# Reordering the split-precision products of a routed feed-forward by kind, and counting several column blocks per product in its routing searches

## The chip, the cores and the metric

The kernel runs on one core of one Trainium2 chip. The metric is the device time of one execution in microseconds, as the median of several runs. The profile and its trace come from one execution, profiled apart from those runs.

## What is computed

Three stages follow each other: causal attention mixed with a memory read-out, a routed feed-forward with eight experts, and a second feed-forward with weights common to all tokens. Cut to what matters, the reference is:

```python
x = attention(q, k, v, M_prev, z_prev, beta)      # 2304 tokens x 512
logits = x @ w_gate                               # 8 experts, 288 places each
order = np.argsort(-logits.flatten())
for idx in order:                                 # best pair of token and expert first
    tok, e = (int(idx) // E, int(idx) % E)
    if assigned[tok] >= 0 or counts[e] >= cap:
        continue
    assigned[tok] = e
    counts[e] += 1
for e in range(E):
    h = np.maximum(x[assigned == e] @ w1[e], 0.0)
    out[assigned == e] = h @ w2[e]
h = np.maximum(np.maximum(x @ w1, x @ w2), x @ w3)   # x is now that out
return h @ w_out
```

## The kernel before

Every matmul of the two feed-forwards has float32 accuracy from three products that add up in one accumulator: an fp32 product of the rounded halves ("hi", line 1429) and two bf16 products with the rests ("lo", lines 1431 and 1432). `mm3` issues the three together, so that TensorE goes hi, lo, lo, hi, lo, lo. Weights are split on the fly: ScalarE rounds (`whi`, line 1370), VectorE subtracts (`wlo`, line 1376), ScalarE copies the rounded half as bf16 (line 1380). The common weights are split once into `mh` and `ml` (lines 1280 to 1295).

The experts are worked through in the order in which they fill up, p = 0 to 7, 288 tokens each. For one expert the kernel gathers its token rows (line 1345), transposes them (line 1405) and splits them. The first feed-forward goes over eight blocks fb of the hidden layer: four triples over d into an accumulator `w` (task "h1", lines 1451 to 1460), a ReLU and a split into `hh` and `hl`, and four triples into the accumulators `acc` (task "y", lines 1480 to 1493). The last two blocks' y products are made together. The second feed-forward (lines 1521 to 1595) goes over six blocks f: three tiles i of four triples each from `yh` and `yl`, of which the maximum `mt` is kept (line 1552), then the output products (`fo`), 512 columns wide. Three accumulators `w` exist.

Between these products runs the routing (`routing`, line 1043). Which expert fills up next, and with which tokens, is found by a search per expert: VectorE compares each token's best logit with a grid of thresholds (`cq`, line 1140), TensorE counts by expert how many tokens lie above each threshold, one product per column block of 128 tokens, 18 in all (line 1148), VectorE compares the counts with the places left (`fl`, line 1152), TensorE sums the flags (line 1158), and VectorE moves the grid (lines 1167 and 1169). `PLANS` has the bits of each step: five steps (7, 5, 5, 5, 6) in the first search, four of 7 bits in the six later ones; the last expert needs none. A search ends with the expert's number (line 1181) and its token list (line 1225); the list is written to memory and read back in another layout on SyncE's queue (`fi` and `fj`, lines 1512 and 1516), which also issues the weight loads `wraw` (line 1361), three buffers deep.

The order on every engine is laid down before the run. `Plan.run` (line 151) takes tasks greedily: the one that can start first by planned costs and latencies, and among equals the one with the smaller key. The keys come from the tables `FK`, `RKEY` and `R1KEY`.

Of the kernel before, what the change touches and what calls it, by code (L numbers as in the profile page):

```python
# [22 lines left out]
F32 = mybir.dt.float32  # L23
# [18 lines left out]
PLANS = ((7, 5, 5, 5, 6), (7, 7, 7, 7))  # L42
# [3 lines left out]
RKEY = (-1000, -23.5)  # L46
FL0 = 3
NFILL = 88
R1, R1KEY = 9, 21.8
NK = 4  # L50
RSLACK = 300
# [4 lines left out]
FK = {"m2": -600, "ml": 28.3, "load": -63.7, "w2": 17.1, "wsplit": -3.5, "gather": -148.1, "xt": -126.2, "h1": 0, "y": -46.8, "o": 13.0, "store": 103.5, "idx": -41.5}  # L56
# [185 lines left out]
def attention(g, tc, ctx, consts, beta, qN, kN, v1, vT, mz, mT, wg, xd, L, m2):  # L242
# [677 lines left out]
    def search():  # L920
# [40 lines left out]
        op("DVE", 65, lambda: V.tensor_scalar(g.st[1], g.pw[1], g.am, None, op0=OP.mult), [t])  # L961
# [81 lines left out]
def routing(g, tc, plan, rt, rps, L):  # L1043
# [33 lines left out]
    es2 = tl("es2", [E])  # L1077
    k, key, slack = [0], [0.0], [0]

# [42 lines left out]
    for ph in range(E):  # L1122
# [7 lines left out]
        if ph < E - 1:  # L1130
            cur, cn = m, "m"
            pl = min(ph, 1)
            n = len(PLANS[pl])
            for s in range(n):
                Z, q, w = 2 ** PLANS[pl][s], CQ[pl], PQ[pl]
                late = ph == 0 and s == 0
                if late:
                    q = w = 3
                for a in range(CE if late else 0, NB, q):
# [10 lines left out]
                    P((30 if ph else 50) * w + (60 if ph else 0), cnt, " ".join(f"cq{x}" for x in range(a + q - w, a + q, q)) + " ohU" +  # L1150
                      (" CNT" if a + q > w or late else " RA"), "CNT")
                V(70, lambda Z=Z: v.tensor_tensor(fl[:Z], CNT[:Z], R[:Z], op=OP.is_ge), "CNT R", "fl")
# [7 lines left out]
                P((54 if base else 27) + 100 * (ph > 0), fpm, "fl", "FP")  # L1160
# [49 lines left out]
        for a in range(0, NB, q):  # L1210
# [10 lines left out]
            r.ti = P((30 if ph else 95) * w + (60 if ph else 0), idx, " ".join(f"cq{x}" for x in range(a + q - w, a + q, q)) + " mov0 mov1 mov2" +  # L1221
# [26 lines left out]
def experts(g, tc, plan, top, wr, xd, idxd, out):  # L1248
# [32 lines left out]
    for k in range(NK, 12):  # L1281
# [3 lines left out]
        def flow(e, k=k, h=0):  # L1285
            if h == 0:
                g.slot(k)
            q = slice(512 * h, 512 * h + 512)
            V.tensor_sub(ML[k][:, 0, q], g.W32[k][:, q], MH[k][:, q].bitcast(F32))

        t = add(FK["m2"] + k, {"ACT": act(1024)}, fh)
        for h in range(2):
            low = add(FK["ml"] + .1 * k + .05 * h, {"DVE": dve(512)}, lambda e, f=flow, h=h: f(e, h=h), [t, low, g.rounds[0].tt])
        low = add(FK["ml"] + .1 * k + .07, {"ACT": act(1024)}, lambda e, k=k: A.copy(ML[k][:, 1], MH[k].bitcast(F32)), [low])
# [36 lines left out]
    for p in range(E):  # L1331
# [95 lines left out]
        def mm3(o, w, r, start, stop, part=(0, 1)):  # L1427
            if 0 in part:
                nc.tensor.matmul(o, w[0], r[0], start=start, stop=False)  # L1429
            if 1 in part:  # L1430
                nc.tensor.matmul(o, w[2], r[1], start=False, stop=False)  # L1431
                nc.tensor.matmul(o, w[1], r[2], start=False, stop=stop)  # L1432

# [11 lines left out]
        ylast, yt = [], []  # L1445
        for fb in range(8):
# [4 lines left out]
            for hf in range(2):  # L1451
                def fh1(e, x=x, fb=fb, hf=hf, o=o):
                    if hf == 0:
                        o.pt = ps.tile([128, 512], F32, name="w", bufs=FBUFS["w"])
                    for d in (2 * hf, 2 * hf + 1):
                        s = slice(d * 128, d * 128 + 128)
                        mm3(o.pt[:, :T], wts(x.W[fb], s), tri(x.xh, x.xl, d), d == 0, d == 3)

                t = add(kh + FK["h1"] + .1 * hf, {"PE": 760}, fh1, x.tw[fb, 0] + (x.tx[:6] if hf == 0 else x.tx + [t]), new=[bp] if hf == 0 else [],
                        use=([] if hf == 0 else [bp]) + x.bx + list(x.bw[fb]))  # L1460
# [19 lines left out]
            for hf, (fb, ts, o, bhh, bhl) in itertools.product(range(2), yt):  # L1480
                def fy(e, x=x, fb=fb, hf=hf, o=o, part=(0, 1)):
                    for d in (2 * hf, 2 * hf + 1):
                        if fb == 0:
                            x.acc[d] = ps.tile([128, 512], F32, name="acc", bufs=4)
                        s = slice(512 + d * 128, 512 + d * 128 + 128)
                        mm3(x.acc[d][:, :T], wts(x.W[fb], s), (o.a, (o.b[:, 0] if 1 in part else None), (o.b[:, 1] if 1 in part else None)), fb == 0, fb == 7, part)

                ky = k0 + 2 * fb + FK["y"] + .1 * hf if fb < 6 else k0 + 14 + FK["y"] + hf + .1 * (fb - 6)
                for part in ((0,), (1,)) if fb == 7 else ((0, 1),):
                    ylast.append(add(ky + .05 * part[0], {"PE": 270 * (0 in part) + 490 * (1 in part)}, lambda e, f=fy, part=part: f(e, part=part),  # L1490
                                     list(ts if 1 in part else ts[:1]) + x.tw[fb, 1] + ylast[-1:] + ([o[-1] for o in prev.ol] if prev else []),
                                     new=ya[2 * hf:2 * hf + 2] if fb == 0 else [],
                                     use=[bhh, bhl] + list(x.bw[fb]) + (ya[2 * hf:2 * hf + 2] if fb else [])))
# [3 lines left out]
        for d in range(4):  # L1497
            def hi(x=x, d=d):
                if not hasattr(x, "yh"):
# [4 lines left out]
                               [ylast[-4 + d // 2 * 3]] + x.ty[:1], new=x.by if d == 0 else [], use=[ya[d]] + ([] if d == 0 else x.by)))  # L1504
# [13 lines left out]
        t = add(k0 + FK["idx"], {"SP": 500}, fi, [r.tt] + x.tl[FL0:FL0 + 1], lat=2300)  # L1518
        x.tidx = add(k0 + FK["idx"] + .1, {"SP": 500}, fj, [t], lat=2300)
        x.tm = []  # L1520
        for f in range(6):
# [3 lines left out]
            for i in range(3):  # L1525
# [3 lines left out]
                for hf in range(2):  # L1529
                    def fp(e, x=x, f=f, i=i, hf=hf, o=o, part=(0, 1)):  # L1530
                        if hf == 0 and 0 in part:
                            o.pt = ps.tile([128, 512], F32, name="w", bufs=FBUFS["w"])
                        for d in (2 * hf, 2 * hf + 1):
                            s = slice(d * F2 + f * 128, d * F2 + f * 128 + 128)
                            mm3(o.pt[:, :T], msub(i, s.start, 128), tri(x.yh, x.yl, d), d == 0, d == 3, part)

                    for part in ((0,), (1,)) if f == 0 and i == 0 else ((0, 1),):
                        need = x.ty[:6] if hf == 0 else x.ty + [t]
                        if part == (0,):
                            need = x.ty[6 * hf:6 * hf + 6:3] + ([t] if hf else [])  # L1540
                        elif part == (1,):
                            need = need + [t]
                        t = tp = add(kf + i + .1 * hf + .05 * part[0], {"PE": 270 * (0 in part) + 490 * (1 in part)},
                                     lambda e, f=fp, part=part: f(e, part=part), need + TM[i], new=[bp] if hf == 0 and 0 in part else [],
                                     use=([] if hf == 0 and 0 in part else [bp]) + x.by)
# [39 lines left out]
            for ci, c in enumerate(chunks):  # L1585
                h, w = (was, 0) if c * 128 < p * T else (own, 128 * (c - full[0]))

                def fo(e, x=x, f=f, ci=ci, h=h, w=w):
# [3 lines left out]
                    mm3(x.oc[ci], [a[:, w:w + 128] for a in (h.t, h.u[:, 0], h.u[:, 1])], msub(3, s.start, DM), f == 0, f == 5)  # L1592
# [121 lines left out]
```

## Time and profile before

| what | value |
|---|---|
| median of 3 runs | 817.12 us (816.01 to 817.22) |
| the profiled execution | 816.3 us |
| its span in the trace | 814.6 us |
| TensorE busy | 783.8 us, 96% of the span |
| VectorE, ScalarE, GpSimd busy | 578.6, 480.7, 107.6 us |
| granted TensorE clock, mean | 0.982 of full speed |
| HBM read, written | 72.77 MB, 9.74 MB |

Attention fills the span up to about 245 us, expert 0's gather begins at 263.6 us, and the last product starts at 807.0 us. Times are counted from the start of the span. Matmuls are pipelined, so the duration of one overlaps the next; the spacing of their starts says how long one holds the engine.

### The profile page before, as it was taken

To read this page: it belongs to the slowest core of one execution; us is meant where nothing else is said; L and a number is where in the kernel's file an instruction comes from. 1 tells how busy PE (TensorE), PEld (TensorE's weight loads), DVE (VectorE), ACT (ScalarE), POOL (GpSimd) and SP (SyncE) were. 2 spreads that over 40 slices of the span, in tenths; PEclk is the share of its full clock that TensorE was granted. 3 is DMA by queue.
4 is the path that set the end of the run, shared out by engine and by line. 5 is a ranking of instruction groups with operands and counts; after the bars stand their busy time and mean duration, and the time that the engine had idled before them with its cause. 6 is when DMAs were issued, how large, how long until landed. Compare 5 with 4: busy or idle time off the path is not lost.

```text
span 814.6 us, 18746 instructions
## 1 busy us (share of the span) xinstructions
PE 783.8 (96%) x7022; PEld 623.4 (77%) x7022; DVE 578.6 (71%) x1780; ACT 480.7 (59%) x1238; POOL 107.6 (13%) x239
## 2 busy tenths in 40 slices
PE   8999999999986799999999999999999999999996
PEld 6899899899985567677777777767767777776773
DVE  7799999999557888688668757747856865643421
ACT  4678777777647673674564655546556465835521
POOL 2212222223101100201010210110101012001001
PEclk9999999999995899999999999999999999999999
DMA  7364746565013422322312320411331253421000
GB/s 239 91 220 153 238 130 233 177 219 169 23 60 93 110 51 79 107 79 96 116 53 79 107 79 30 157 54 39 104 107 54 78 134 107 132 25 52 2 1 39
DMA packets 39248, 83.79 MB, mean 103 GB/s; under 512 B 11454, under 2 KB 14198, under 8 KB 39158
## 3 DMA queue, kind: packets, MB, share of 16 engines
q1 hardware_dynamic: 35574, 72.87, 28.8%
q0 software_dynamic: 3584, 9.73, 4.0%
q8 instruction: 55, 0.90, 0.5%
q14 instruction: 35, 0.29, 0.1%
HBM read 72.77 MB, written 9.74 MB: 101 GB/s over the span
## 4 chain that ended last, share of the span: by engine, by line
PE 73%; issue 9%; DVE 8%; DMA 5%; ACT 3%; POOL 1%; SPq 1%; DVEq 0%; POOLq 0%; ACTq 0%
PE w L1431 12%; PE w L1429 12%; PE w L1432 11%; PE av L684 9%; PE acc L1429 6%; PE acc L1431 6%; PE acc L1432 5%; PE st L643 5%; PE rps L590 2%; PE rps L1148 2%; PE rps L543 1%; DMA wraw<-in_wr 1%; DVE junk L456 1%; DMA m2raw<-in_m2w 1%; PE w L1405 1%
## 5 line engine op out<-in xcount | busy, mean ns | idle before, releaser
L1429 PE MATMUL w<-yh,mh 128*128 128x288 f32 x576 | 219.8, 390 | 0.2 <-DVE mt L1552 0.2
L1431 PE MATMUL w<-yl,ml 128*128 128x288 bf16 x576 | 169.4, 296 | 0.0
L1432 PE MATMUL w<-yl,ml 128*128 128x288 bf16 x576 | 163.7, 286 | 0.0
L1429 PEld LDWEIGHTS w<-yh,mh 128*128 128x128 f32 x576 | 107.6, 190 | 17.9 <-DVE mt L1552 0.6
L684 PE MATMUL av<-V,pt 128*128 128x112 f32 (+1 forms) x960 | 105.0, 261 | 1.7 <-DVE nm L456 0.7
L684 PEld LDWEIGHTS av<-V,pt 128*128 128x128 f32 (+1 forms) x960 | 96.9, 173 | 6.4 <-issue 1.6
L1429 PE MATMUL w<-xhi,whi 128*128 128x288 f32 x256 | 100.3, 392 | 0.5 <-DVE xlo L1321 0.5
L1429 PE MATMUL acc<-hh,whi 128*128 128x288 f32 x256 | 95.9, 385 | 0.1
L1376 DVE TENSOR_TENSOR wlo<-wraw,whi 128x512 bf16<-128x512 f32 x128 | 84.2, 686 | 15.2 <-ACT whi L1370 14.4
L1552 DVE TENSOR_TENSOR mt<-w,mt 128x288 f32<-128x288 f32 x96 | 43.7, 455 | 66.3 <-PE w L1432 62.2
L1431 PEld LDWEIGHTS <-ml 128*128 128x128 bf16 x576 | 55.0, 96 | 39.0 <-issue 7.2
L1370 ACT CAST whi<-wraw 128x512 fp32r<-128x512 f32 x128 | 74.5, 617 | 17.4 <-PE acc L1429 9.1
L1431 PE MATMUL w<-xlo,wlo 128*128 128x288 bf16 x256 | 76.8, 300 | 1.9 <-ACT wlo L1380 1.9
L1380 ACT CAST wlo<-whi 128x512 bf16<-128x512 f32 x128 | 76.2, 616 | 0.0
L1431 PEld LDWEIGHTS <-wlo 128*128 128x128 bf16 x512 | 49.4, 96 | 34.4 <-ACT wlo L1380 2.4
L1431 PE MATMUL acc<-hl,wlo 128*128 128x288 bf16 x256 | 75.7, 298 | 0.0
L1432 PE MATMUL w<-xlo,wlo 128*128 128x288 bf16 x256 | 74.0, 289 | 0.0
L456 DVE CUSTOM_DVE_ANT_0 junk<-st,mask 128x512 bf16<-128x512 f32 (+3 forms) x128 | 62.6, 489 | 15.6 <-ACT pt L668 3.8
L1432 PE MATMUL acc<-hl,wlo 128*128 128x288 bf16 x256 | 73.1, 288 | 0.1
L1345 POOL DMA_INDIRECT xg<-xd,tidx x24 | 30.1, 1253 | 255.7 <-PE w L1432 233.3
L670 ACT ACTIVATE pt<-st 128x512 f32<-128x512 f32 x96 | 53.3, 601 | 14.2 <-PE st L643 13.2
L1432 PEld LDWEIGHTS <-ml 128*128 128x128 bf16 x576 | 57.1, 99 | 0.6
(283 smaller groups left out, 1699.2 us busy)
## 6 DMA issues: line engine op xcount, KB each, us to landing
wraw<-in_wr SPq DMA_DIRECT2D x64, 512.0 KB, 4.3
m2raw<-in_m2w SPq DMA_DIRECT2D x12, 512.0 KB, 5.2
V<-in_v SPq DMA_DIRECT2D x16, 365.0 KB, 5.3
KR<-in_kN SPq DMA_DIRECT2D x16, 288.0 KB, 3.1
QN<-in_qN SPq DMA_DIRECT2D x16, 288.0 KB, 3.1
vt<-in_vT SPq DMA_DIRECT2D x16, 288.0 KB, 5.1
xd<-x SPq DMA_DIRECT2D x16, 256.0 KB, 2.5
m2raw<-in_m2w SPq DMA_DIRECT2D x12, 256.0 KB, 3.1
```

Of the source, the lines that this page charges most:

```text
L456: V.tensor_tensor_reduce(out=junk[:, :w], in0=o.s[x][:, c:c + w], in1=m, scale=1.0, scalar=-3.0e38, op0=OP.add, op1=OP.max, accum_out=r.nm ...
L643: PE.matmul(d[:kr, c:c + z - a], neg[q, :kr] if wt is None else wt[q, k], mv[q, a:z], start=x == 0, stop=x == 3)
L670: A.activation(r.PT[:, i, 512 * gi:512 * gi + 512], o.t[i], AF.Exp, scale=0.125)
L684: PE.matmul(AV[:m, i, j * C:j * C + w], r.PT[:, i, o:o + m], r.V[:, c:c + w], start=kb == 0, stop=kb == j)
L1345: g.gather = G.indirect_dma_start(out=x.xg[:96, c], out_offset=None, in_=xd, in_offset=bass.IndirectOffsetOnAxis(ap=r.tidx[:96, c:c + 1], ...
L1370: A.copy(x.W[fb][0][:, q], x.RAW[fb][:, q])
L1376: V.tensor_sub(x.W[fb][1][:, 0, q], x.RAW[fb][:, q], x.W[fb][0][:, q].bitcast(F32))
L1380: A.copy(x.W[fb][1][:, 1, q], x.W[fb][0][:, q].bitcast(F32))
L1429: nc.tensor.matmul(o, w[0], r[0], start=start, stop=False)
L1431: nc.tensor.matmul(o, w[2], r[1], start=False, stop=False)
L1432: nc.tensor.matmul(o, w[1], r[2], start=False, stop=stop)
L1552: V.tensor_max(q.mt, o.pt[:, :T], q.mt)
```

## The change

Three things are done. First, `mm3` becomes `mms`, which issues either the hi products of a group or its lo products, and the tasks h1, y and those of the second feed-forward are cut by kind: all four hi of a block, then its eight lo; in `HALF` cases two hi, four lo, twice. Each part waits only for what it reads. The y products of the last two blocks follow a list, `YSEQ`. Second, the later searches use the five-step plan too, and in all steps but the first they count G = 4 (5 bits) or 2 (6 bits) column blocks in one product: the thresholds of G blocks are the stationary operand, the expert flags of G blocks the moving one, a mask keeps the matching pieces, VectorE reduces them by expert, and a product with `fold` adds the pieces. The mask and fold are made on GpSimd. Third, one low copy of common weights (k = 4) is made by a DMA from GpSimd's queue, the index transfers of expert 0 wait for its last weight load, and the tables of keys and planned costs are new.

```diff
-PLANS = ((7, 5, 5, 5, 6), (7, 7, 7, 7))
+PLANS = ((7, 5, 5, 5, 6),)
-RKEY = (-1000, -23.5)
+RKEY = (-1000, -51.2)
-R1, R1KEY = 9, 21.8
+R1, R1KEY = 9, 16.6
+YSEQ = ((0, 0, (0, 1, 2, 3)), (0, 1, (0, 1)), (1, 0, (0, 1)), (1, 1, (0, 1)), (0, 1, (2, 3)), (1, 0, (2, 3)), (1, 1, (2, 3)))
...
+                if ph and s:
+                    G = 128 // Z
...
+                    V(60 + 1.05 * NB * Z, lambda cp=cp, k=kst[pl][:, s - 1], cur=cur, Z=Z: v.tensor_tensor(
+                        cp[:, :NB * Z].rearrange("p (x z) -> p x z", z=Z), cur[:, :, None].to_broadcast([128, NB, Z]),
+                        k[:, None, :Z].to_broadcast([128, NB, Z]), op=OP.is_ge), f"{cn} kst{pl}{s}", names)
...
+                        for x in xs:
+                            w = min(G, NB - x)
+                            nc.tensor.matmul(C4[:w * Z, :w * E], cp[:, x * Z:(x + w) * Z], o[:, x * E:(x + w) * E], start=(x == 0), stop=(x == xs[-1]))
...
+                    V(90, lambda C4=C4, G=G: v.tensor_mul(c4[:, :E * G], C4, mask[G]), "C4", "c4")
+                    V(85, lambda G=G: v.tensor_reduce(c1, c4[:, :E * G].rearrange("p (a e) -> p e a", a=G), axis=AX.X, op=OP.max), "c4", "c1")
+                    P(50, lambda C1=C1, G=G: nc.tensor.matmul(C1, fold[G], c1, start=True, stop=True), "c1", "C1")
+                    V(70, lambda C1=C1, Z=Z: v.tensor_tensor(fl[:Z], C1, R[:Z], op=OP.is_ge), "C1 R", "fl")
...
+                G.dma_start(ML[k][:, 1], MH[k].bitcast(F32))
...
-        def mm3(o, w, r, start, stop, part=(0, 1)):
-            if 0 in part:
+        ALL, HALF = ((0, (0, 1, 2, 3)), (1, (0, 1, 2, 3))), ((0, (0, 1)), (1, (0, 1)), (0, (2, 3)), (1, (2, 3)))
+
+        def mms(part, o, w, r, start, stop):
+            if part == 0:
                 nc.tensor.matmul(o, w[0], r[0], start=start, stop=False)
-            if 1 in part:
+            else:
                 nc.tensor.matmul(o, w[2], r[1], start=False, stop=False)
                 nc.tensor.matmul(o, w[1], r[2], start=False, stop=stop)
...
-            for hf in range(2):
-                def fh1(e, x=x, fb=fb, hf=hf, o=o):
...
+            for n, (part, ds) in enumerate(HALF if fb == 0 and p == 0 else ALL):
+                def fh1(e, x=x, fb=fb, o=o, part=part, ds=ds):
...
+            seq = [(i, part, ds) for i in range(len(yt)) for part, ds in (HALF if fb == 0 else ALL)]
+            if fb == 7:
+                seq = YSEQ
...
-        t = add(k0 + FK["idx"], {"SP": 500}, fi, [r.tt] + x.tl[FL0:FL0 + 1], lat=2300)
-        x.tidx = add(k0 + FK["idx"] + .1, {"SP": 500}, fj, [t], lat=2300)
+        t = add(k0 + FK["idx"], {"SP": 500}, fi, [r.tt] + (x.tl[FL0:FL0 + 1] if p else x.tl[7:]), lat=11000)
+        x.tidx = add(k0 + FK["idx"] + .1, {"SP": 500}, fj, [t], lat=5000)
...
-                for hf in range(2):
-                    def fp(e, x=x, f=f, i=i, hf=hf, o=o, part=(0, 1)):
+                for n, (part, ds) in enumerate(HALF if f == 0 else ALL):
+                    def fp(e, x=x, f=f, i=i, o=o, part=part, ds=ds):
```

What this does to the order is shown at three places, in rows of the built programs. The first is TensorE in the second feed-forward, where `yh` and `yl` are the split tokens and `mh` and `ml` the split common weights; an fp32 product brings its weight load along, a bf16 one has it in a row of its own. Before, two triples of a block:

```order
L1429 MATMUL w<-yh,mh_4128 128x288
L1431 LDWEIGHTS ml
L1431 MATMUL w<-yl,ml 128x288
L1432 LDWEIGHTS ml
L1432 MATMUL w<-yl,ml 128x288
L1429 MATMUL w<-yh,mh_4129 128x288
L1431 LDWEIGHTS ml
L1431 MATMUL w<-yl,ml 128x288
```

Now, two blocks that stand together:

```order
L1471 MATMUL w<-yh,mh_1161 128x288
L1471 MATMUL w<-yh,mh_1436 128x288 x2
L1471 MATMUL w<-yh,mh_1699 128x288
L1471 MATMUL w<-yh,mh_4135 128x288
L1471 MATMUL w<-yh,mh_4136 128x288 x2
L1473 LDWEIGHTS ml_998
L1473 MATMUL w<-yl,ml_998 128x288
L1474 LDWEIGHTS ml_998
L1474 MATMUL w<-yl,ml_998 128x288
```

The hi products have moved ahead of the lo ones of their block, here of two blocks, and sixteen lo follow; runs of eight hi of the second feed-forward stand at 40 places.

The second place is TensorE in a packed step of a search, where `cq` holds the comparisons and `ohU` the expert flags. Before, the last of eighteen count products and what follows:

```order
L1148 LDWEIGHTS cq
L1148 MATMUL rps<-ohU,cq 128x8
L1429 MATMUL acc<-hh,whi 128x288
L1431 LDWEIGHTS wlo
L1431 MATMUL acc<-hl,wlo 128x288
```

Now the first two of five, which stand between the hi and the lo of a y task, and further down the fold:

```order
L1471 MATMUL acc<-hh,whi 128x288 x4
L1162 LDWEIGHTS cq
L1162 MATMUL rps<-ohU,cq 128x32
L1162 LDWEIGHTS cq
L1162 MATMUL rps<-ohU,cq 64x16
```

```order
L1471 MATMUL w<-xhi,whi 128x288 x4
L1471 MATMUL acc<-hh,whi 128x288 x4
L1167 MATMUL rps<-c_4095,fold_4102 32x8
L1473 LDWEIGHTS wlo
L1473 MATMUL w<-xlo,wlo 128x288
```

Thirteen products of the step are gone; a fold product has come, behind the eight lo of the y task and eight more hi.

The third place is SyncE's queue in expert 0, where `wraw` are the weight loads and `idxd` and `idx` the two index transfers. Before:

```order
L1361 DMA wraw<-in_wr 128x1024
L1512 DMA idxd<-tidx 96x3x1
L1361 ISA
L1361 DMA wraw<-in_wr 128x1024
L1516 DMA idx<-idxd 128x2x1
L1361 ISA
L1361 DMA wraw<-in_wr 128x1024
L1337 TENSOR_LOAD ei
```

Now:

```order
L1401 DMA wraw<-in_wr 128x1024
L1401 ISA
L1401 DMA wraw<-in_wr 128x1024
L1401 ISA
L1401 DMA wraw<-in_wr 128x1024
L1565 DMA idxd<-tidx 96x3x1
L1569 DMA idx<-idxd 128x2x1
L1377 TENSOR_LOAD ei
```

Both index transfers have moved behind the last of the eight weight loads, and stand together ahead of the read of the next expert's number.

## Rows read from the trace of the kernel before

**Rows 1.** The page's first part: busy us, share of the span, instructions.

```profile
PE 783.8 (96%) x7022; PEld 623.4 (77%) x7022; DVE 578.6 (71%) x1780; ACT 480.7 (59%) x1238; POOL 107.6 (13%) x239
```

**Rows 2.** Busy time by stretch: us, engines' busy us, granted clock, DMA share, GB/s.

```profile
268.00:305.00 37.00, 32.84 (x257) 24.60 (x258) 30.14 (x60) 28.20 (x58) 0.96 (x1) 0.86 0.39 83
305.00:768.00 463.00, 462.69 (x3793) 345.46 (x3793) 312.55 (x929) 261.92 (x649) 42.24 (x52) 1.00 0.26 82
...
296.00:300.00 4.00, 4.00 (x21) 2.81 (x19) 3.78 (x8) 4.00 (x9) 0.00 (x0) 0.57 0.00 0
```

**Rows 3.** Waits, 255 to 815 us: engine, releaser, total us, times, longest.

```profile
DVE mt L1552 <- PE w L1432: 62.2, 47, 3.7
...
POOL xg L1345 <- DVE R L1245: 16.2, 1, 16.2
...
PE rps L1157 <- DVE fl L1152: 0.2, 1, 0.2
```

**Rows 4.** Timeline of TensorE, expert 7: start us, us, line, out<-in, form, count.

```profile
765.22 0.39 PE L1429 MATMUL acc<-hh,whi 128*128 128x288 f32 x1
765.46 0.30 PE L1431 MATMUL acc<-hl,wlo 128*128 128x288 bf16 x1
765.59 0.29 PE L1432 MATMUL acc<-hl,wlo 128*128 128x288 bf16 x1
765.62 0.39 PE L1429 MATMUL acc<-hh,whi 128*128 128x288 f32 x1
...
766.01 0.51 PE L1429 MATMUL acc<-hh,whi 128*128 128x288 f32 x2
...
766.50 0.29 PE L1432 MATMUL acc<-hl,wlo 128*128 128x288 bf16 x1
766.62 0.29 PE L1431 MATMUL acc<-hl,wlo 128*128 128x288 bf16 x1
...
766.77 0.65 PE L1429 MATMUL w<-yh,mh 128*128 128x288 f32 x3
767.26 0.30 PE L1431 MATMUL w<-yl,ml 128*128 128x288 bf16 x1
```

**Rows 5.** Timeline of TensorE: filling products; one set of count products and the next.

```profile
262.78 2.62 PE L1301 MATMUL acc<-ones 128*128 128x128 bf16 x44
...
281.32 0.60 PE L1148 MATMUL rps<-ohU,cq 128*128 128x8 bf16 x18
281.78 0.38 PE L1429 MATMUL acc<-hh,whi 128*128 128x288 f32 x1
```

**Rows 6.** Timeline of TensorE in attention: a run of fp32 products and the next.

```profile
99.83 2.06 PE L684 MATMUL av<-V,pt 128*128 128x112 f32 x17
101.66 0.48 PE L440 MATMUL st<-KH,qj 128*128 128x512 f32 x1
```

**Rows 7.** Timeline of SyncE's queue, expert 0.

```profile
279.66 0.43 SPq L1512 DMA_DIRECT2D idxd<-tidx  x1
282.56 0.35 SPq L1361 DMA_DIRECT2D wraw<-in_wr  x1
288.93 0.40 SPq L1516 DMA_DIRECT2D idx<-idxd  x1
289.58 44.42 SPq L1361 DMA_DIRECT2D wraw<-in_wr  x7
```

**Rows 8.** Timelines of ScalarE and of TensorE in expert 0; idle us and releaser last.

```profile
261.75 1.90 ACT L1370 CAST whi<-wraw 128x512 fp32r<-128x512 f32 x3 [5.64 <-DMA wraw<-in_wr]
...
292.74 1.14 ACT L1370 CAST whi<-wraw 128x512 fp32r<-128x512 f32 x2 [2.28 <-DMA wraw<-in_wr]
...
295.40 0.30 PE L1431 MATMUL w<-xlo,wlo 128*128 128x288 bf16 x1 [1.59 <-ACT wlo L1380]
```

**Rows 9.** The page's costliest groups: weight loads, busy us and mean ns of one.

```profile
L1429 PEld LDWEIGHTS w<-yh,mh 128*128 128x128 f32 x576 | 107.6, 190 | 17.9 <-DVE mt L1552 0.6
...
L1431 PEld LDWEIGHTS <-ml 128*128 128x128 bf16 x576 | 55.0, 96 | 39.0 <-issue 7.2
```

More of the change, by code (lines that the diff above doesn't have):

```diff
@@ L1077, in routing @@
     es2 = tl("es2", [E])
+    c4, c1 = tl("c4", [4 * E]), tl("c1", [E], F32R)
     k, key, slack = [0], [0.0], [0]
+    mask, fold = {}, {}
+    for n in (2, 4):
+        z = 128 // n
+        mask[n], fold[n] = tl(f"mask{n}", [E * n], BF), tl(f"fold{n}", [z], F32R)
+        nc.gpsimd.memset(mask[n], 0.0)
+        for a in range(n):
+            nc.gpsimd.memset(mask[n][z * a:z * a + z, E * a:E * a + E], 1.0)
+    nc.gpsimd.tensor_add(fold[2], g.ident[:, :64], g.ident[:, 64:])
+    nc.gpsimd.tensor_add(fold[4], fold[2][:, :32].bitcast(F32), fold[2][:, 32:].bitcast(F32))
     def at():
@@ L1148, in cnt @@
                             nc.tensor.matmul(CNT[:Z], cq[:, x, :Z], ohU[:, x], start=(x == 0), stop=(x == NB - 1))
-                    P((30 if ph else 50) * w + (60 if ph else 0), cnt, " ".join(f"cq{x}" for x in range(a + q - w, a + q, q)) + " ohU" +
+                    P((27 if ph else 50) * w + (30 if ph else 0), cnt, " ".join(f"cq{x}" for x in range(a + q - w, a + q, q)) + " ohU" +
                       (" CNT" if a + q > w or late else " RA"), "CNT")
-                V(70, lambda Z=Z: v.tensor_tensor(fl[:Z], CNT[:Z], R[:Z], op=OP.is_ge), "CNT R", "fl")
+                if not (ph and s):
+                    V(70, lambda Z=Z: v.tensor_tensor(fl[:Z], CNT[:Z], R[:Z], op=OP.is_ge), "CNT R", "fl")
                 base = s in (0, n - 1)
@@ L1219, in idx @@
                     nc.tensor.matmul(IX[:z], cq[:, x, :z], mov[:, x], start=(x == 0), stop=(x == NB - 1))
-            r.ti = P((30 if ph else 95) * w + (60 if ph else 0), idx, " ".join(f"cq{x}" for x in range(a + q - w, a + q, q)) + " mov0 mov1 mov2" +
+            r.ti = P((27 if ph else 95) * w + (30 if ph else 0), idx, " ".join(f"cq{x}" for x in range(a + q - w, a + q, q)) + " mov0 mov1 mov2" +
               (" IX" if a + q > w else ""), "IX")
@@ L1285, in flow @@
         def flow(e, k=k, h=0):
-            if h == 0:
+            if k not in ML:
                 g.slot(k)
@@ L1291, in experts, with fhb @@
         t = add(FK["m2"] + k, {"ACT": act(1024)}, fh)
[L1292 to L1294 removed]
+        if k == NK:
+            def fhb(e, k=k):
+                g.slot(k)
+                G.dma_start(ML[k][:, 1], MH[k].bitcast(F32))
+            hb = add(-699, {"POOL": 1100}, fhb, [t], lat=8000)
+        for h in range(2):
+            low = add(FK["ml"] + .1 * k + .05 * h, {"DVE": dve(512)}, lambda e, f=flow, h=h: f(e, h=h), [t, low, g.rounds[0].tt] + ([hb] if k == NK else []))
+        if k > NK:
+            low = add(FK["ml"] + .1 * k + .07, {"ACT": act(1024)}, lambda e, k=k: A.copy(ML[k][:, 1], MH[k].bitcast(F32)), [low])
+        else:
+            TM[k // 3].append(hb)
         TM[k // 3].append(low)
@@ L1450, in experts @@
             t = None
-            for hf in range(2):
-                def fh1(e, x=x, fb=fb, hf=hf, o=o):
-                    if hf == 0:
+            for n, (part, ds) in enumerate(HALF if fb == 0 and p == 0 else ALL):
+                def fh1(e, x=x, fb=fb, o=o, part=part, ds=ds):
+                    if not hasattr(o, "pt"):
                         o.pt = ps.tile([128, 512], F32, name="w", bufs=FBUFS["w"])
-                    for d in (2 * hf, 2 * hf + 1):
+                    for d in ds:
                         s = slice(d * 128, d * 128 + 128)
-                        mm3(o.pt[:, :T], wts(x.W[fb], s), tri(x.xh, x.xl, d), d == 0, d == 3)
-                t = add(kh + FK["h1"] + .1 * hf, {"PE": 760}, fh1, x.tw[fb, 0] + (x.tx[:6] if hf == 0 else x.tx + [t]), new=[bp] if hf == 0 else [],
-                        use=([] if hf == 0 else [bp]) + x.bx + list(x.bw[fb]))
+                        mms(part, o.pt[:, :T], wts(x.W[fb], s), tri(x.xh, x.xl, d), d == 0, d == 3)
+                need = x.tw[fb, 0][:1] + [x.tx[3 * d] for d in ds]
+                if part:
+                    need = x.tw[fb, 0] + [y for d in ds for y in x.tx[3 * d:3 * d + 3]]
+                t = add(kh + FK["h1"] + .05 * n, {"PE": cost(part, ds)}, fh1, need + [t], new=[] if n else [bp],
+                        use=([bp] if n else []) + x.bx + list(x.bw[fb]))
             def ha(o=o):
@@ L1479, in experts, with fy @@
                 continue
[L1480 to L1483, printed above, removed]
+            seq = [(i, part, ds) for i in range(len(yt)) for part, ds in (HALF if fb == 0 else ALL)]
+            if fb == 7:
+                seq = YSEQ
+            for n, (i, part, ds) in enumerate(seq):
+                yb, ts, o, bhh, bhl = yt[i]
+                def fy(e, x=x, fb=yb, o=o, part=part, ds=ds):
+                    for d in ds:
+                        if fb == 0 and part == 0:
                             x.acc[d] = ps.tile([128, 512], F32, name="acc", bufs=4)
                         s = slice(512 + d * 128, 512 + d * 128 + 128)
[L1486 to L1493, printed above, removed]
+                        mms(part, x.acc[d][:, :T], wts(x.W[fb], s), (o.a, o.b[:, 0] if part else None, o.b[:, 1] if part else None), fb == 0, fb == 7)
+                ky = k0 + 2 * yb + FK["y"] + .05 * n if fb < 7 else k0 + 14 + FK["y"] + .1 * n
+                ylast.append(add(ky, {"PE": cost(part, ds)}, fy, (list(ts) + x.tw[yb, 1] if part else [ts[0], x.tw[yb, 1][0]]) + ylast[-1:] +
+                                 ([o[-1] for o in prev.ol] if prev else []), new=[ya[d] for d in ds] if yb == 0 and part == 0 else [],
+                                 use=[bhh, bhl] + list(x.bw[yb]) + ([ya[d] for d in ds] if yb or part else [])))
+                for d in ds:
+                    x.yd[d] = ylast[-1]
             yt = []
@@ L1528, in experts @@
                 t = None
-                for hf in range(2):
-                    def fp(e, x=x, f=f, i=i, hf=hf, o=o, part=(0, 1)):
-                        if hf == 0 and 0 in part:
+                for n, (part, ds) in enumerate(HALF if f == 0 else ALL):
+                    def fp(e, x=x, f=f, i=i, o=o, part=part, ds=ds):
+                        if not hasattr(o, "pt"):
                             o.pt = ps.tile([128, 512], F32, name="w", bufs=FBUFS["w"])
-                        for d in (2 * hf, 2 * hf + 1):
+                        for d in ds:
                             s = slice(d * F2 + f * 128, d * F2 + f * 128 + 128)
[L1535 to L1545, printed above, removed]
+                            mms(part, o.pt[:, :T], msub(i, s.start, 128), tri(x.yh, x.yl, d), d == 0, d == 3)
+                    need = [y for d in ds for y in x.ty[3 * d:3 * d + 3]] if part else [x.ty[3 * d] for d in ds]
+                    t = tp = add(kf + i + .05 * n, {"PE": cost(part, ds)}, fp, need + [t] + TM[i], new=[] if n else [bp],
+                                 use=([bp] if n else []) + x.by)
                 def fm(e, i=i, o=o, q=q):
@@ L1591, in fo @@
                     s = slice(f * DM, f * DM + DM)
-                    mm3(x.oc[ci], [a[:, w:w + 128] for a in (h.t, h.u[:, 0], h.u[:, 1])], msub(3, s.start, DM), f == 0, f == 5)
+                    for part in range(2):
+                        mms(part, x.oc[ci], [a[:, w:w + 128] for a in (h.t, h.u[:, 0], h.u[:, 1])], msub(3, s.start, DM), f == 0, f == 5)
                 x.ol[ci].append(add(kf + FK["o"] + .1 * ci, {"PE": 665}, fo, h.ts + TM[3] + x.ol[ci][-1:],
```

24 lines of the change are left out of this document (16 added, 8 removed).

## The prediction, made before the changed kernel ran

> **What bounds the kernel now.** I read the page's engine table first, then busy time by stretch, then the list of waits, then TensorE's timeline at the scale of single products. The table [rows 1] has TensorE busy for 96% of the span and nothing else above 77%. [...] The waits [rows 3] agree: VectorE waits for TensorE (62.2 us, 47 times), while TensorE waited for a threshold flag of the search once, 0.2 us. The attention stage keeps its order; the change leaves 0 to 255 us alone.
>
> **Term 1, products in order of kind.** A product of three is one fp32 matmul (hi) and two bf16 ones (lo). In [rows 4] a lone triple runs 0.24 us from its hi to its first lo, 0.13 to the second and 0.03 to the next hi: 0.39 to 0.40 us a triple, two in 0.79 (765.22 to 766.01). Where the kernel already puts two hi ahead of four lo, those two triples take 0.76 (766.01 to 766.77). Inside runs, hi follows hi after 0.13 (three and the way to their lo in 0.49, 766.77 to 767.26) and lo follows lo after 0.12 (766.50 to 766.62). A block of four, four hi then eight lo, is then 0.24 + 3 x 0.13 + 0.13 + 6 x 0.122 + 0.03 = 1.52 us against 4 x 0.391 = 1.56: 0.04 for three fewer crossings from hi to lo, 14 ns each. The pair says up to 0.03 per crossing, with rows that resolve 0.01. I take 14 ns and keep 10 and 20 as ends. How many crossings go is counted in the two orders, from the first gather transpose to the last product: 1150 become 300, since the schedule also sets two blocks' hi together (40 runs of eight fp32 products in the second feed-forward) and lets an output product's hi join a run. 850 x 14 ns = **11.9 us less** (8.5 to 17), all of it on the path where TensorE is full.
>
> **Term 2, counting several column blocks in one product.** Of the seven searches six are late ones, and each did 4 x 18 count products. Eighteen take 0.46 us (281.32 to 281.78, [rows 5]), 25.5 ns each, so 1.84 us a search. Now there are 18, then 5 + 5 + 5 and 9: 42, at 1.07 us if 16 or 32 output columns cost what 8 do. The trace has no such product; the nearest other one is the 128-column bf16 matmul, 44 in 2.62 us, 60 ns each [rows 5], which would add 0.8 us. New are four fold products (fp32, 8 columns) and one more threshold sum. No row shows a fold; it lies between 25 ns (the bf16 one of 8 columns) and 108 ns (attention's fp32 products of 112 columns, 17 in 1.83 us from 99.83 to 101.66, [rows 6]). I take 60 ns, between both: 0.24 + 0.03. New sum 1.34, saving 0.5 us x 6 = **3.0 us less** (1.0 to 3.4). VectorE's grid compares shrink from twelve of 128x768 to three of those, three of 576 and one of 1152 elements, while each of the four packed steps gains a mask product and a reduction. That is fewer microseconds on an engine with 150 to spare, so nothing outside expert 0. The chain of one search is longer, five steps and four extra trips through TensorE, but it still ends before the second feed-forward begins, so a whole feed-forward lies between the choice of the next expert and that expert's first product; late next would be its gather.
>
> **Term 3, the index store on the load queue.** In [rows 7] SyncE stores expert 0's indices at 279.66, issues the seventh weight load at 282.56, and then stands at the index load until the store has landed, 288.93. The eighth weight load, queued behind it, goes out only at 289.58. ScalarE then idles 2.28 us for those weights, to 292.74 [rows 8]. TensorE waits 1.59 us for the lo half, to 295.40, and after that gap the granted clock averages 0.57 from 296 to 300 us [rows 2], 4 x 0.43 = 1.7 us lost. The change puts both index transfers behind all eight loads of expert 0. Up to 1.59 + 1.7 + 0.3 = 3.6 us goes; nothing, if ScalarE, nearly full here, is late anyway. The row nearest is its 2.28 us of idleness, so I take **3.0 us less**. From expert 1 on the same wait exists but TensorE is full there, so moving it is worth 0.
>
> **What costs nothing.** GpSimd gains eight memsets, two additions and a bf16 copy by DMA, all ahead of the first gather. It sits idle 16.2 us before that gather [rows 3], which covers them; without that cover each microsecond would delay expert 0 by one. The scalings and the low copy dropped from ScalarE lie before its idle time of 5.64 us that ends at 261.75 [rows 8]: 0 either way. The one scaling dropped from VectorE stands before that, with ScalarE's grid waiting on the scaling that stays: 0.
>
> **Term 4, given back.** With eight hi in a row the schedule needs the first block's accumulator (three tiles, w) free eight lo and four hi after its last product, 8 x 0.122 + 4 x 0.13 = 1.5 us, where one block at a time gave two blocks, 3.1 us. The copy out is 0.46 us on VectorE, and in 47 of 96 cases VectorE was waiting for it [rows 3]; in the rest it came to it late. I take **1.5 us more** (0 to 6).
>
> **Sum.** The profiled execution took 816.3 us (span 814.6). 816.3 - 11.9 - 3.0 - 3.0 + 1.5 = 799.9. The median of the runs is 817.1, 0.8 above it, so **800.7 us**. By the ends: 794 where crossings give 20 ns, 809 where term 1 gives 8.5, term 2 gives 2 and term 3 nothing, with 2 to 3 us given back.
>
> **Rivals.** *More is returned (15%).* VectorE and ScalarE come late to the closely spaced pairs, and TensorE stops for accumulators or for folds, which stand in its queue and hold the products behind them. At 0.15 us for each of the 40 runs of eight, 6 us, it gives 805 to 808. For it: the shorter allowance of term 4. Against: 0.2 us of waiting for flags in the whole expert stage.
>
> *More is won (10%).* 20 ns a crossing and all of term 3: 794.
>
> *The fp32 weight load comes into view (3%): slower.* Before, each hi load (190 ns, against 96 for bf16, [rows 9]) mostly ran under a bf16 product. In runs of hi it must run under a 0.13 us product. If from the fourth hi of a run on each waited for its whole load, 190 instead of 133 ns, the 611 such hi of the new order would cost 35 us, and the kernel takes 835. It decides from 27 ns each on (16.4 us / 611). Against it: the runs of three hold 0.13, and attention's 17 fp32 products stand 108 ns apart with loads of the same kind [rows 6], so a load does not need its recorded time.
> [...]
>
> *The change does not do what it says.* The order excludes this: hi and lo stand in runs, and count products drop to 42.
>
> **Chances.** Forecast 70%, more returned 15%, more won 10%, fp32 loads 3%, and 2% for a search that ends too late or a stall I have not seen, near 817. The first three are all faster, so faster by over 0.2% (1.6 us, about what a measurement of this kernel tells from no change) 0.94, within it 0.02, slower 0.04. The range 794 to 809 leaves out the slow cases and the far edges.
>
> **What would show it.** Right: a stretch of a block of four in 1.52 us; TensorE full through experts 1 to 7 with the mean of these seven (463 / 7 = 66 us) down by 2 us; count products in 1.1 us a search; ScalarE without the 2.28 us gap and the clock at 1.00 from 296 to 300. Wrong: hi spaced over 0.15 us in runs, new TensorE waits for mt, c1 or fl, or expert 0 ending its first feed-forward no earlier against the start of its gather.

## The result, and the profile after

The changed kernel takes 805.43 us (median of four runs, 804.69 to 806.21); the kernel before, beside it, 817.17 us. The ratio is 0.9857 [0.9839, 0.9874]: 11.7 us less, where 16.4 were forecast, and inside the range of 794 to 809. The profiled executions are 816.3 and 805.9 us. The missing 5 us are not where the prediction looked for losses.

The page's engine table of the changed kernel (columns as in [rows 1]):

```profile
PE 775.2 (96%) x6848; PEld 645.9 (80%) x6872; DVE 555.7 (69%) x1795; ACT 482.6 (60%) x1250; POOL 112.2 (14%) x246
```

Its busy time by stretch (columns as in [rows 2]):

```profile
268.00:305.00 37.00, 33.27 (x257) 26.54 (x258) 30.34 (x69) 30.96 (x63) 0.98 (x1) 0.91 0.27 83
305.00:768.00 463.00, 461.55 (x3698) 369.87 (x3718) 292.78 (x943) 264.38 (x666) 46.43 (x52) 1.00 0.29 82
296.00:300.00 4.00, 3.78 (x32) 3.00 (x30) 3.27 (x8) 4.00 (x8) 0.00 (x0) 1.00 0.03 0
```

From expert 1 on TensorE is as full as before, so its spacings are again the time. The clock dip of 296 to 300 us is gone, 1.00 where it was 0.57.

The list of waits of the changed kernel (whole span):

```profile
ACT mt L1597 <- PE w L1474: 47.1, 26, 4.3
DVE mt L1599 <- PE w L1474: 46.5, 29, 3.1
...
PE w L1473 <- ACT wlo L1420: 1.1, 2, 0.8
```

VectorE and ScalarE still wait for TensorE at the maximum `mt`. TensorE waits for ScalarE's low weights 1.1 us in all, in expert 0; from 305 to 768 us the list names no wait of TensorE.

TensorE's timeline of the changed kernel, two paired blocks of the second feed-forward (columns as in [rows 4]):

```profile
377.78 1.30 PE L1471 MATMUL w<-yh,mh 128*128 128x288 f32 x8
378.92 0.30 PE L1473 MATMUL w<-yl,ml 128*128 128x288 bf16 x1
379.06 0.29 PE L1474 MATMUL w<-yl,ml 128*128 128x288 bf16 x1
...
380.77 0.29 PE L1474 MATMUL w<-yl,ml 128*128 128x288 bf16 x1
380.80 0.39 PE L1471 MATMUL w<-yh,mh 128*128 128x288 f32 x1
```

Eight hi reach their first lo in 1.14 us (seven steps of 0.13 and a crossing of 0.23), and eight whole triples take 3.02 us, 0.378 each, against 0.39 to 0.40 for a lone one in [rows 4]. That is term 1 as predicted. The next two places of the same timeline are not as predicted:

```profile
344.29 0.29 PE L1474 MATMUL w<-xlo,wlo 128*128 128x288 bf16 x1
344.42 0.48 PE L1162 MATMUL rps<-ohU,cq 128*128 128x32 bf16 x5
344.74 0.28 PE L1473 MATMUL w<-xlo,wlo 128*128 128x288 bf16 x1
...
355.30 0.29 PE L1473 MATMUL acc<-hl,wlo 128*128 128x288 bf16 x1
355.42 0.29 PE L1474 MATMUL acc<-hl,wlo 128*128 128x288 bf16 x1
355.64 0.17 PE L1189 MATMUL rps<-fl,ones 32*128 32x8 bf16 x1
355.74 0.66 PE L1471 MATMUL w<-xhi,whi 128*128 128x288 f32 x3
```

Five packed count products hold the engine 0.32 us (344.42 to 344.74), 64 ns each, where eighteen of before took 25.5 ns each [rows 5]. The flag sum, a product over 32 rows (`32*128`), starts 0.22 us after the lo ahead of it, which otherwise holds the engine 0.12, and the next hi starts 0.10 later.

To sum this over the span I took each group of search products that stands between two expert products, from 272 us on, and subtracted from its stretch what the same neighbours take without it. In each kernel one flag sum over 1 us, where TensorE waited, is left out. "Padded" is the kernel with both paddings, below.

| group (how often; mean ns) | before | changed | padded |
|---|---|---|---|
| 18 counts of one block | 24; 549 | 6; 525 | 6; 529 |
| 5 counts of four blocks | – | 18; 358 | 18; 160 |
| 9 counts of two blocks | – | 6; 226 | 6; 227 |
| fold | – | 24; 66 | 24; 74 |
| flag sum alone | 11; 114 | 17; 274 | 17; 95 |
| low bits and flag sum, or pairs of both | 16; 111 | 6; 139 and 6; 517 | 6; 139 and 6; 172 |
| sum, us | 16.2 | 21.1 | 12.7 |

The searches take 4.9 us more of TensorE than before, not 3.0 less. Their counts gave back 2.2 us, the folds took 1.6, and the flag sums, with the low bits, 5.6.

### The profile page after: what moved, and what is told of

It reads as the page before. It is cut to its first block, busy times and chain, and to the rows that moved or that the text cites. A ratio compares the mean times of both kernels' runs of the same rounds, so it can differ in the third digit from the quotient of the medians.

```text
span 804.2 us, 18456 instructions
## 1 busy us (share of the span) xinstructions
PE 775.2 (96%) x6848; PEld 645.9 (80%) x6872; DVE 555.7 (69%) x1795; ACT 482.6 (60%) x1250; POOL 112.2 (14%) x246
## 4 chain that ended last, share of the span: by engine, by line
PE 77%; issue 10%; DVE 7%; ACT 3%; POOL 1%; DMA 1%; DVEq 0%; POOLq 0%; ACTq 0%
PE w L1471 13%; PE w L1473 11%; PE w L1474 11%; PE av L685 10%; PE acc L1471 6%; PE acc L1474 6%; PE acc L1473 5%; PE st L644 5%; PE rps L591 2%; DVE junk L457 2%; PE rps L544 2%; PE w L1445 1%; PE rps L1178 1%; PE rps L1162 1%; PE st L444 1%
## 5 line engine op out<-in xcount | busy, mean ns | idle before, releaser
L1473 PE MATMUL w<-yl,ml 128*128 128x288 bf16 x576 | 146.0, 287 | 0.0
L1474 PE MATMUL w<-yl,ml 128*128 128x288 bf16 x576 | 145.2, 286 | 0.0
L1471 PE MATMUL w<-yh,mh 128*128 128x288 f32 x576 | 102.9, 314 | 0.0
L1471 PEld LDWEIGHTS w<-yh,mh 128*128 128x128 f32 x576 | 82.0, 189 | 4.0
L457 DVE CUSTOM_DVE_ANT_0 junk<-st,mask 128x512 bf16<-128x512 f32 (+3 forms) x128 | 62.5, 488 | 15.5 <-ACT pt L669 3.7
L1385 POOL DMA_INDIRECT xg<-xd,tidx x24 | 33.9, 1414 | 248.2 <-issue 177.8
L1473 PE MATMUL w<-xlo,wlo 128*128 128x288 bf16 x256 | 66.1, 289 | 1.1 <-ACT wlo L1420 1.1
L1473 PE MATMUL acc<-hl,wlo 128*128 128x288 bf16 x256 | 66.8, 288 | 0.0
L1474 PE MATMUL acc<-hl,wlo 128*128 128x288 bf16 x256 | 66.2, 286 | 0.0
L1474 PE MATMUL w<-xlo,wlo 128*128 128x288 bf16 x256 | 65.7, 287 | 0.0
L1359 DVE SCALAR_TENSOR_TENSOR hl<-w,hh 128x288 bf16<-128x288 f32 x64 | 29.1, 455 | 44.4 <-ACT hh L1353 44.0
L1353 ACT ACTIVATE hh<-w 128x288 fp32r<-128x288 f32 x64 | 26.2, 410 | 54.2 <-PE w L1474 53.9
```

The costliest lines, as they stand in the source:

```text
L457: V.tensor_tensor_reduce(out=junk[:, :w], in0=o.s[x][:, c:c + w], in1=m, scale=1.0, scalar=-3.0e38, op0=OP.add, op1=OP.max, accum_out=r.nm ...
L1385: g.gather = G.indirect_dma_start(out=x.xg[:96, c], out_offset=None, in_=xd, in_offset=bass.IndirectOffsetOnAxis(ap=r.tidx[:96, c:c + 1], ...
```

## Experiments

On each chip the kernel before ran beside the others; it took 816.7 to 818.8 us there, so I compare ratios to it, and 0.001 is 0.8 us. The changed kernel ran a second time as a mark.

> The changed kernel once more, unaltered, as the mark for the three others on the same chip: 0.986 of the kernel before, 0.984 to 0.988.

Measured: 0.9870 [0.9848, 0.9893]. Its two ratios, 0.9857 and 0.9870, are what the others stand against.

**The narrow products.** Two edits fill up the array with zeros. In the flag path the fold gets zero columns up to 128, and flags and flag sums go over 128 rows:

```diff
-mask[n], fold[n] = tl(f"mask{n}", [E * n], BF), tl(f"fold{n}", [z], F32R)
+mask[n], fold[n] = tl(f"mask{n}", [E * n], BF), tl(f"fold{n}", [128], F32R)
+nc.gpsimd.tensor_sub(fold[n][:, z:], g.ident[:, :128 - z], g.ident[:, :128 - z])
...
-v.tensor_tensor(fl[:Z], C1, R[:Z], op=OP.is_ge)
+v.tensor_tensor(fl, C1, R, op=OP.is_ge)
...
+if ph and s:
+    Z = 128
```

In the packed counts the last piece is full (`ohX` is `ohU` with two zero blocks behind it):

```diff
-o = ohU.rearrange("p x e -> p (x e)")
+o = g.ohX.rearrange("p x e -> p (x e)")
...
-w = min(G, NB - x)
+w = G
```

> The changed kernel with its searches' TensorE products padded to the whole array: the two last column blocks that are missing from the packed count are added as zeros, so that every count product has 128 columns; the fold is 128 columns wide (zeros beyond the 32 or 64); the threshold flags are made over 128 partitions and summed over 128. No arithmetic is added to the path; each product only uses more rows or columns of the array.
> [...]
> Rival (the switch of shape costs nothing; the products wait for VectorE's longer chain): the clusters keep their time, 805 to 806 us.

> The changed kernel with the padding of the fold and the flag sums alone (128 partitions); the packed counts stay as changed, their last piece 64 columns wide in the steps of 32 thresholds.
> Theory (each return from a product of fewer rows has its own price): the flag sums 321 to some 110 ns (18) and the last pairs 517 to 170 ns (6) give back 3.8 + 2.1 = 5.9 us of the 9 us that the whole padding won: ratio to before 0.979 to 0.981.
> Rival (one narrow product in a step is enough to pay all of it, so that only the whole padding helps): 0.985 to 0.988.

> The changed kernel with the padding of the packed counts alone (two zero blocks, so that the last piece of the steps of 32 thresholds is 128 columns wide); fold and flag sums stay as changed.
> Theory: the counts of 32 columns fall from 358 to 160 ns (18): 3.6 us less, ratio to before 0.981 to 0.984.
> Rival (as above): 0.985 to 0.988.

Measured: both 0.9747 [0.9733, 0.9761], 797.68 us against 818.78; flags alone 0.9794 [0.9781, 0.9808]; counts alone 0.9815 [0.9801, 0.9830]. The same places in the timeline of the kernel with both:

```profile
343.35 0.29 PE L1477 MATMUL w<-xlo,wlo 128*128 128x288 bf16 x1
343.47 0.28 PE L1163 MATMUL rps<-ohX,cq 128*128 128x32 bf16 x5
343.60 0.28 PE L1476 MATMUL w<-xlo,wlo 128*128 128x288 bf16 x1
...
353.75 0.29 PE L1476 MATMUL acc<-hl,wlo 128*128 128x288 bf16 x1
353.88 0.29 PE L1477 MATMUL acc<-hl,wlo 128*128 128x288 bf16 x1
354.00 0.17 PE L1192 MATMUL rps<-fl,ones 128*128 128x8 bf16 x1
354.03 0.65 PE L1474 MATMUL w<-xhi,whi 128*128 128x288 f32 x3
```

The five counts now hold 0.13 us instead of 0.32, though one of them has become larger. The flag sum follows its lo after 0.12 instead of 0.22, and the next hi follows it after 0.03 instead of 0.10. The gain over the changed kernel is 0.011 to 0.012, 9 to 10 us (8.4 by the table, and 7.8 to 8.5 if the times from the different chips are compared as they stand). The two parts, 0.006 to 0.008 and 0.004 to 0.006, add up to the whole. For both together the estimate before the run, from the group means, was 9 us less, 795 to 799 us (3.7 for the flag sums, 2.4 for the last pairs and 3.6 for the counts, which make 9.7); all three results fell in their estimated ranges and outside the rivals'. So the shape of these products is the cause: they do the same sums, and only the zeros were added. This version beats both kernels.

**The old searches in the changed kernel.**

```diff
-PLANS = ((7, 5, 5, 5, 6),)
+PLANS = ((7, 5, 5, 5, 6), (7, 7, 7, 7))
...
-pl, pc = 0, min(ph, 1)
+pl, pc = min(ph, 1), min(ph, 1)
...
-if ph and s:
+if False:
```

> The changed kernel with the old searches of experts 1 to 6 (four steps of 128 thresholds, 18 count products each, no fold); the order of the products in kinds and all else as changed.
> Theory (the new searches cost TensorE more than the old ones, +2.8 us by the traces): 802 to 803.5 us, faster than the changed kernel.
> The prediction's second term (the new searches save 3.0 us): about 808.5 us. Rival (the searches lie beside TensorE's other work, whatever their products): within 1 us of 805.4.

Measured: 0.9878 [0.9860, 0.9895], 808.57 us where the kernel before took 818.78. Against the changed kernel's ratios that is 0.001 to 0.002 more, with intervals that overlap: the theory missed, and the prediction's 3 us are not there either. The list of TensorE's waits from 300 to 800 us in this kernel tells why that alone decides nothing:

```profile
PE acc L1465 <- ACT hh L1347: 1.4, 3, 0.5
PE acc L1467 <- DVE hl L1353: 1.4, 2, 1.0
PE rps L1244 <- DVE cq L1236: 1.3, 4, 0.4
```

The planner's keys belonged to the new searches, so the old ones stood in the wrong places: 4.1 us in these three waits, and the granted clock averaged 0.57 from 570 to 574 us. So I put them back at the keys of before as well (`RKEY` -23.5, `R1KEY` 21.8).

> The changed kernel with the old searches, and with their steps' keys (RKEY, R1KEY) of before as well; the first try kept the new keys, and its trace shows TensorE waiting for VectorE's thresholds in expert 4, where the clock fell once (570.5 to 573.9 us).
> Theory (the new searches cost TensorE some 2 to 3 us more than the old ones): 2 us less than the changed kernel, ratio 0.983 to 0.984.
> Prediction's second term: 3 us more, 0.989 to 0.990.

Measured: 0.9810 [0.9791, 0.9829], 800.83 us, and on the same chip the changed kernel had 0.9870: 0.006, 4.9 us less. The prediction's second term fell, with the opposite sign; the theory's 2 us were too few. TensorE's waits from 300 to 800 us are 1.4 us in this kernel and none in the changed one.

**The order by kind.** `mms` was made to issue triples again, `ALL` to hold two halves of triples.

```diff
-if part == 0:
+if part != 1:
     nc.tensor.matmul(o, w[0], r[0], start=start, stop=False)
-else:
+if part:
     ...
```

> The changed kernel with the expert products in triples again (high, low, low for each slice); the new searches and the index transfers as changed.
> Theory (the first term: some 14 ns for each return from a low product to a high one, 850 of them and more): about 816.5 us, range 814 to 818, thus level with the kernel before or a little slower than it less its other gains.
> Rival (the order of kinds is worth less, and the start of expert 0 or the schedule gave the gain): 806 to 811 us.

Measured: 1.0100 [1.0083, 1.0116], about 20 us above the changed kernel: outside both ranges. The second try, whose expectation gives waits for the rounded hidden units as the reason, restored what had gone with the triples:

> The expert products in triples again, this time with all that went with them before: the split of the last slice of hidden units and of the first gate product into high and low parts, and the keys of the planner's steps (table FK) of before. New searches and new index place stay. The first try at triples lost 20 us against the changed kernel, and its trace shows why it was no clean test: the second product waited in each expert for the rounded hidden units (0.46 and 0.49 us), since the order of triples did not have that split.
> Theory (some 14 ns for each return from a low product to a high one, 830 more of them by the traces: 11.6 us, and stalls of the mixed schedule made the other 8): 11 to 13 us more than the changed kernel, a ratio to the kernel before of 1.000 to 1.003.
> Rival (order by kind is worth more than the crossings, since it also covers waits): 16 us more or worse, 1.006 and up.

Measured: 1.0075 [1.0057, 1.0092], 0.0205 or 16.7 us above the changed kernel on that chip. The rival's number, not the theory's. Those waits are too small to be the reason: in the first try TensorE waited for `hh` four times from 300 to 800 us, 1.2 us in all, 0.3 at most. To see whether the narrow products made the excess, the same edit was made in the padded kernel:

> The padded kernel (counts, fold and flag sums over the whole array) with the expert products in triples, with the splits and the planner's keys of before, as in the second try at the order.
> Theory (16.5 us that the second try lost were 12 us for the crossings and 4 to 5 us for the narrow search products, which cost more between triples): against the padded kernel's 0.975 the loss is 12 to 13 us, ratio 0.989 to 0.991.
> Rival (the order of kinds is worth 16 us whatever the searches): 0.994 to 0.996.

Measured: 0.9958 [0.9944, 0.9971], 0.0211 or 17 us above the padded kernel: the rival again, so padding explains none of it. The traces of the two padded kernels split it. From the first product on `yh` of expert 6 to that of expert 7 no routing product stands on TensorE. This stretch takes 62.41 us in triples and 60.84 by kind, with 143 and 32 crossings from hi to lo: 1.57 us / 111 = 14.1 ns. For the whole stage (1157 and 300 crossings) that is 12.1 us. The other part lies in the groups of routing products, index products included, which add some 23 us in triples and 19 by kind, about 4 us more; together that is 16 of the 17 us. TensorE's timeline in triples:

```profile
345.12 0.29 PE L1477 MATMUL w<-xlo,wlo 128*128 128x288 bf16 x1
345.24 0.28 PE L1163 MATMUL rps<-ohX,cq 128*128 128x32 bf16 x5
345.37 0.38 PE L1474 MATMUL w<-xhi,whi 128*128 128x288 f32 x1
345.58 0.30 PE L1476 MATMUL w<-xlo,wlo 128*128 128x288 bf16 x1
```

From last lo to next lo this takes 0.46 us. Without the counts the same neighbours take 0.26 (0.03 to the hi and 0.23 to its lo, [rows 4]). The five counts cost 0.20 us here (0.21 in most groups) between a lo and a hi, but 0.13 between two lo, as in the padded kernel's 343.47 to 343.60. Groups of 18 counts show the same: in the kernel with the old searches at their old place they cost 538 ns between lo and hi, 450 between hi and lo. In triples nearly every group stands ahead of a hi; by kind, half of them do not. The 85 ns are the same for five products, for eighteen and for a single flag sum (113 and 28 ns in the padded kernel), so they belong to the place and not to a product. The rows point at the lo ahead: it holds the engine 0.03 us where a hi follows and 0.12 where a count does, while the hi behind the counts needs 0.21 to its lo, hardly less than 0.23. Why that is so was not tried apart.

**The index transfers.** Put back in the changed kernel, and moved alone in the kernel before:

```diff
-t = add(k0 + FK["idx"], {"SP": 500}, fi, [r.tt] + (x.tl[FL0:FL0 + 1] if p else x.tl[7:]), lat=11000)
-x.tidx = add(k0 + FK["idx"] + .1, {"SP": 500}, fj, [t], lat=5000)
+t = add(k0 + FK["idx"], {"SP": 500}, fi, [r.tt] + x.tl[FL0:FL0 + 1], lat=2300)
+x.tidx = add(k0 + FK["idx"] + .1, {"SP": 500}, fj, [t], lat=2300)
```

> The changed kernel with the index transfers of the experts at their old places on SP's queue (the dependences and latencies of before, for all experts); all else as changed.
> Theory (the third term: behind them the weight loads of expert 0 arrive late, ScalarE stands idle for about 2.3 us and TensorE's clock dips once): 807 to 808.5 us.
> Rival (the order of the products leaves enough cover for the late loads): 805 to 806 us.

> The kernel before with the one change of the index transfers' place on SP's queue (dependences and latencies of the change), nothing else.
> Theory A (the third term as predicted, the place alone frees ScalarE's weight rounding): 3 us less than before, expert 0 from first gather transpose to its first gate product 33 us instead of 35.9, ratio 0.996 to 0.997.
> Theory B (what putting the transfers back into the changed kernel showed: 0 to 1 us; expert 0 was shortened by something else, the order by kind or the fourth resident weight's copy that left ScalarE for a transfer): ratio 0.999 to 1.001.

Measured: back in the changed kernel 0.9866 [0.9846, 0.9886], no difference from 0.9857 and 0.9870, so the rival holds; the interval alone would leave room for about 2 us, and the traces of expert 0 below speak against them. Moved alone in the kernel before 0.9956 [0.9940, 0.9972], 3.6 us less, so theory A holds. Both are right at once. The changed kernel with the old place, SyncE's queue and ScalarE:

```profile
278.29 0.42 SPq L1565 DMA_DIRECT2D idxd<-tidx  x1
288.28 0.41 SPq L1569 DMA_DIRECT2D idx<-idxd  x1
289.28 2.20 SPq L1401 DMA_DIRECT2D wraw<-in_wr  x2
...
292.29 1.05 ACT L1332 CAST ml<-mh 128x1024 bf16<-128x1024 f32 x1
293.59 0.62 ACT L1410 CAST whi<-wraw 128x512 fp32r<-128x512 f32 x1 [0.25 <-DMA wraw<-in_wr]
```

The weight load goes out as late as in [rows 7], at 289.28, but ScalarE lacks it for 0.25 us only, not 2.28 [rows 8]: the planner set the copy of a common weight (1.05 us) and other work ahead of it. In the kernel before with the transfers moved, ScalarE runs on:

```profile
289.77 1.14 ACT L1380 CAST wlo<-whi 128x512 bf16<-128x512 f32 x2
290.81 1.14 ACT L1370 CAST whi<-wraw 128x512 fp32r<-128x512 f32 x2
```

Expert 0, from its first gather transpose to its first product on `yh`, took 37.4 us before (268.18 to 305.58), 34.4 with the transfers moved alone, 35.4 in the changed kernel and 35.1 there with them put back. The 35.9 and 33 us of the expectation are not what these rows give, but their difference is. What covers the late load in the changed kernel, the order by kind, the new keys or the low copy that a DMA now makes, was not tried apart.

## Why the prediction was right or wrong

- **What bounds.** Right: TensorE from expert 1 on, busy 461.55 of the 463 us from 305 to 768 at a granted clock of 1.00, so that its spacings are the time there, as in [rows 2]; in expert 0 ScalarE stands beside it (30.96 of 37 us busy).
- **Term 1** was right in mechanism and size: 14.1 ns a crossing where 14 were taken, 12.1 us where 11.9 were. What it left out is the cheaper place for routing products, some 4 us by the padded pair. The sign that was named, seven experts 2 us shorter in the mean, came by half: from the first product on `yh` of expert 0 to that of expert 7 it is 454.1 us where it was 461.2, 1.0 us an expert; with the old searches at their old place it is 448.2 us, 1.9 an expert.
- **Term 2** is the step that failed: "42, at 1.07 us if 16 or 32 output columns cost what 8 do", with 0.03 us for one more threshold sum. The moving columns did cost nothing: nine counts of 16 columns take 226 ns, five of 32 take 0.13 us once they are padded. The other side of the array cost: the last count piece fills 64 of 128 columns and the flag sums 32 or 64 of 128 rows, and by the table each of these costs about 0.2 us more than padded (a flag sum alone 274 ns against 95, the five counts 358 against 160). With the fold, sized at 60 ns and measured at 66, the searches take 4.9 us more than before by the table, instead of 3.0 less, and 4.9 us more than the old ones in the changed kernel by the run. That the two agree is partly chance: among products in order of kind the old searches hold TensorE about 14 us, 7 less than the new ones, and the 1.4 us of waits stand against that. Padded they take 3.5 us less than before by the table, near the predicted saving, and the padded kernel stands 0.006 below the one with the old searches at their old place, on another chip.
- **What term 2 could have read.** Its range, 1.0 to 3.4 us less, did not hold its own bound: 0.8 us more a search, at 60 ns a packed count, makes the searches 1.8 us dearer. And the flag sums stood in it as one more of 0.03 us, with their rows unregarded. No row I used had a bf16 product with fewer rows or columns, but the trace of the kernel before has some, in its first search. TensorE's timeline there, at a granted clock of 0.50:

```profile
255.71 0.17 PE L1157 MATMUL rps<-low,ones 128*128 128x8 bf16 x1 [0.25 <-DVE fl L1152]
255.81 0.18 PE L1158 MATMUL rps<-fl,ones 64*128 64x8 bf16 x1
255.93 0.19 PE L1163 MATMUL rps<-low,ones 128*128 128x8 bf16 x1
...
258.07 0.17 PE L1194 MATMUL rps<-scn,tri 128*128 128x2 bf16 x1 [0.66 <-DVE scn L1192]
258.10 0.17 PE L1195 MATMUL rps<-scn,ones 128*128 128x1 bf16 x1
```

  A flag sum over 64 rows starts 0.10 us after the product ahead and holds the engine 0.12; two products over 128 rows stand 0.03 apart. The kind of loss, if not its size between the expert products, could be seen before the change ran.
- **What makes the price** no row shows: the flag sums and the 64-column count piece cost about 0.2 us each more than padded, but not every narrow product does. The fold, with 32 columns or padded to 128, holds the engine 0.12 us either way, as the two timelines show (changed, then padded).

```profile
412.16 0.26 PE L1167 MATMUL rps<-c,fold 128*32 128x8 f32 x1
412.28 0.30 PE L1473 MATMUL w<-xlo,wlo 128*128 128x288 bf16 x1
```

```profile
409.76 0.26 PE L1168 MATMUL rps<-c,fold 128*128 128x8 f32 x1
409.88 0.30 PE L1476 MATMUL w<-xlo,wlo 128*128 128x288 bf16 x1
```

- **Term 3** was right for the kernel before (3.6 us where 3.0 were taken) and wrong as a term of the sum: the changed kernel covers the late load as well, so the two gains overlap. Expert 0 became 2.0 us shorter, and 2.3 with the transfers put back.
- **Term 4**, 1.5 us given back in waits for accumulators, did not come: no wait of TensorE stands in the list for experts 1 to 7.
- **The rivals.** The time lies where "more is returned" put it (805 to 808), but by another mechanism: the products themselves became dearer, and from expert 1 on TensorE did not stop for VectorE. The fp32 weight load stayed out of view; hi follow each other after 0.13 us in runs of eight, with a recorded load of 189 ns, almost the 190 of [rows 9].
- **The sum as measured.** Order, index place and all else without the new searches: 0.0190 of 816.7, 15.5 us. The searches gave 4.9 back: 10.6, and the profiled executions differ by 10.4. Terms 1, 3 and 4 together had 13.4; the miss is term 2. That the time still lies inside the range is partly luck: term 2 was off by 7.9 us, and the other parts made up 2.1 of them, with 15.5 instead of 13.4.

## What to carry to other kernels

Before packing or shrinking a TensorE product in a stretch where TensorE is full, compare its rows and columns of the array with those of its neighbours: here a bf16 product over 32 rows or 64 columns cost about 0.2 us more than the same one padded with zeros. The trace may have a product of the new shape in another stage: look for it before a price is taken from the nearest full one. When one schedule covers a late transfer, moving that transfer too gained nothing more here, so gains from one stage should not be summed unseen. An experiment that undoes one part of a planned schedule needs the keys that belonged to that part, or it measures the misplacement.

## What the runs showed of the hardware that was not expected

- A bf16 product over 32 of 128 rows between expert products: 0.22 us after the lo ahead and 0.10 to the next hi, against 0.12 and 0.03 over 128 rows. One product of 64 columns among five: 0.32 us for the five, against 0.13. An fp32 product of 32 columns, the fold: 0.12 us to the next lo, and 0.12 over 128 columns.
- Five small bf16 products cost 0.21 us between a lo and a hi but 0.13 between two lo; eighteen cost 538 ns between a lo and a hi and 450 between a hi and a lo.
